# Transformer layer with memory-augmented attention on one core: the layernorm of the next tile issued a chunk ahead, the gates with the constants, the second-layer weight loads later

## The chip, the cores and the metric

The kernel runs on one core of a Trainium2 chip. The metric is the device time of one execution in microseconds (us). TensorE (PE in the profile, PEld for its weight loads) does the matmuls, ScalarE (ACT) exponentials, gelu and copies, VectorE (DVE) and GpSimd (POOL) the elementwise work, and SyncE (SP) issues nearly all transfers.

## The reference

The input is x with 2048 tokens of 576 values, in bfloat16. Both blocks are pre-normalised and added to their input:

```
h  = x + A(layernorm(x))          # attention with a memory, 32 heads of 18
h2 = h + B(layernorm(h))          # gelu(y @ w1 + b1) @ w2 + b2, 4608 wide
# A: q,k,v = y@wq, y@wk, y@wv; four segments of 512 tokens, in order
logits = q k^T * 18**-0.5 + causal mask          # within the segment
a_dot  = softmax(logits) v
a_mem  = (phi(q) M) / (phi(q) z + 1e-6)          # phi(t) = t+1 if t>0 else exp(t)
o      = g * a_mem + (1-g) * a_dot               # g = sigmoid(beta), one a head
M, z   = M + phi(k)^T v, z + sum(phi(k))         # after each segment
A      = concat(o) @ wo
```

## The kernel before

The tokens are cut into 8 chunks of 256, each of two tiles of 128. Streams written as Python generators describe the work. `stream_P` (one for each tile position `tl`) loads a tile of x, normalises it (`layernorm`: L307 statistics, L311 and L312 on VectorE, the power L317 on GpSimd, L320 on VectorE), transposes it into `xT` and makes q, k and v from it (L300 and L301 with `wqkv`; evictions L383, L386, L388, L391). For the first two chunks the transposes are matmuls (L327, L408) with a copy behind them (L365, L411); later they are DMA transposes (L132). `stream_M` sums phi(k) with v into the memory. `stream_A` does the attention of a chunk in 80 visits: 16 score matmuls (L489), one exp over four banks (L495), the causal mask on GpSimd (L499), 16 small matmuls with v (L518), then the division (L554 to L563) and, from chunk 2 on, the memory part (L528 to L548). `stream_B` transposes the attention output `o_nat` into `xT`, multiplies by `wo` (L635), adds x (L637), and normalises again. `stream_F1` is the first layer (L731, eviction L733, gelu L741) and loads `w1` anew for each chunk in nine groups of 512 columns, into two buffers and, early on, into the unused `hT` buffer; `stream_F2` is the second layer (L767) with `w2` held in `w_sb`.

A planner inside the kernel runs these streams while the program is built. Each operation has an engine, an assumed duration, the operations that it depends on and a due time (the planner's clock plus a value of `SLACK`). An engine that is free takes, of its operations that are ready, the one with the earliest due time; TensorE's operations come from the streams in a fixed priority, with L790 to L795 choosing between the attention streams and the two layers. Where nothing is ready and the first layer has not begun, a filler matmul is issued that nothing reads (L805). The order found in this way is what each engine then executes, strictly in order; the assumed durations have no part in the execution. Transfers use eight semaphores in turn, so SP can issue a transfer only when the eighth before it has landed. Transfers on SP also stand in the planned order.

The buffers that matter here: `x_p[tl]` and `xn1[tl]` (the loaded tile and its normalised form) are single for each tile position; there are three `xT` buffers, and three PSUM banks with `ox` as a fourth where attention doesn't hold it. In `stream_P` before, chunk c is loaded and normalised when its turn has come:

```
yield need(lambda: c < 3 or c - 2 - (c + 1) % 2 in done_A, idle=False)
...
if c > 1:
    load_x(t, xt, xk, SLACK["xp"])
if c > 0:
    layernorm(who, xt[:], xk, xn1[tl], xnk, False, SLACK["lnp"])
```

The gates (L278 to L290: an exp on ScalarE, then seven VectorE operations that make g, 1-g and the masked g) are issued when both tiles of chunk 0 have their q, k and v. `beta` is loaded by a DMA that GpSimd issues (L258). The loads of `w2` and of three groups of `w1` stand in a list `later`, from which `stream_A` takes one at each visit (L593).

Of the kernel before, what the change touches and what calls it, by code (L numbers as in the profile page):

```python
# [8 lines left out]
ACT = mybir.ActivationFunctionType  # L9
# [7 lines left out]
def kernel(  # L17
# [40 lines left out]
    def sbuf(name, shape, dt=BF16):  # L58
# [7 lines left out]
    TP, TB = 2, 1  # L66
    NEVER = 1e9
    TABLE_LOAD = 1.283
    SLACK = dict(head=0, lnp=5.5, lnb=9.5, pow=-8.5, apply=8, ek_k=23, relu_k=40, min_k=5, add_k=9, mz=5, exp=13.5,
                 ek=7.5, relu=7.5, min=9.5, add=-6.5, hb=11.5, gelu=3.5, finish=0.5, mem=-20.5, sum=-7, out=22,  # L70
                 hd=9.5, xp=-15.5, xb=2, t_x=9.5, t_q=74.5, t_k=25.5, t_o=4, t_h=30.5, w1=3, w2=30, hc=21, evict=0,
                 qk=-13, ot=-13, mask=10.5, lead=1.25, balance=21)
    ops = []
    now, dma_free, table = 0.0, 0.0, "exp"
    free_at = {"PE": 0.0, "SP": 0.0, "ACT": 0.0, "DVE": 0.0, "POOL": 0.0}
    port_until = {"DVE": 0.0, "POOL": 0.0}
    queue = {e: [] for e in free_at}
    writer, readers = {}, {}

    class Op:  # L80
        start, end = None, NEVER

        def __init__(self, eng, dur, issue, preds, due, table=None, after=None):
            self.eng, self.dur, self.issue, self.preds, self.due, self.table = eng, dur, issue, preds, due, table
            self.made = len(ops)
            self.after = after

        def seen(self, eng):
            return self.end if self.eng == eng else self.end + LAT[self.eng]

        def ready(self):
            return max((o.seen(self.eng) for o in self.preds), default=0.0)

    def preds_of(rd, wr):
        out = [writer[k] for k in rd if k in writer]
# [4 lines left out]
        return out  # L100

    def ready(eng, rd=(), wr=()):
        return max((o.seen(eng) for o in preds_of(rd, wr)), default=0.0)

    def note(o, rd, wr):
        for k in wr:
            writer[k] = o
            readers[k] = []
        for k in rd:
            readers.setdefault(k, []).append(o)  # L110
# [43 lines left out]
    class Slots:  # L154


        def __init__(self, name, n):
            self.free = [(name, i) for i in range(n)]

        def when(self):  # L160
            return min((ready("PE", (), [k]) for k in self.free), default=NEVER)

        def take(self):
            k = min(self.free, key=lambda k: ready("PE", (), [k]))
            self.free.remove(k)
            return k

# [48 lines left out]
    banks["ox"] = ox  # L216
    bank_slots = Slots("bank", 3)
    bank_slots.free.append("ox")
    LATER, AHEAD = 0, 5
    f_slots = bank_slots  # L220
    xT_slots = Slots("xT", 3)

# [14 lines left out]
    def memset(eng, dur, ap, value, key, slack=0.0):  # L237
        e = nc.vector if eng == "DVE" else nc.gpsimd
        op(eng, dur, lambda: e.memset(ap, value), (), [key], slack)
# [6 lines left out]
        load_x(2 + tl, x_b[tl], ("x_b", tl))  # L246
    weights(wo_t, slice(0, D), A_wo, "wo")

    def constants():
        op("POOL", 0.75, lambda: make_identity(nc, ident[:]), (), ["ident"])  # L250
        op("DVE", 0.27, lambda: nc.vector.memset(pq[:], 0.0), (), ["pq"])
        memset("DVE", 0.06, mhalf[:], -0.5, "mhalf")
        for tl in range(2):
            memset("DVE", 0.09, xn1[tl][:, D:XW], 0.0, ("xn1", tl, "pad"))
        for tl in range(2):
            memset("DVE", 0.46, qk_pads[tl][:, :, Dh:32], 0.0, ("qk", tl, "pad"))
        memset("POOL", 1.53, wqkv[64:KTAIL, 4, :], 0.0, "wqkv_pad")
        op("POOL", 0.75, lambda: nc.gpsimd.dma_start(out=beta_bc[:], in_=A_beta.partition_broadcast(P)), (), ["beta"])  # L258
        for j in range(2):
            memset("DVE", 0.09, v_augs[j][:, :, Dh:E], 1.0, ("v1", j))  # L260
        for tl in range(2):
            layernorm(f"p{tl}", x_p[tl][:], ("x_p", tl), xn1[tl], ("xn1", tl), False, -5)
        for j in range(2, 6):
            memset("DVE", 0.14, v_augs[j][:, :, Dh:E], 1.0, ("v1", j), slack=4)
        memset("DVE", 0.09, maskcol[:], 0.0, "maskcol", slack=5)
        for i in range(4):
            memset("DVE", 0.09, maskcol[32 * i:32 * i + Dh, :], 1.0, "maskcol", slack=5)
        for j in range(2):
            memset("POOL", 0.45, phik_pads[j][:, :, Dh:32], 0.0, ("phik", j, "pad"), slack=5)
        for j in range(2):  # L270
# [7 lines left out]
    def gates():  # L278
        op("ACT", 0.25, lambda: nc.scalar.activation(out=g_bc[:], in_=beta_bc[:], func=ACT.Exp, scale=-1.0), ["beta"], ["g"],
           slack=2, table="exp")  # L280
        op("DVE", 0.18, lambda: nc.vector.tensor_scalar(out=g_bc[:], in0=g_bc[:], scalar1=1.0, scalar2=None, op0=ALU.add), (), ["g"],
           slack=3)
        op("DVE", 0.36, lambda: nc.vector.reciprocal(out=g_bc[:], in_=g_bc[:]), (), ["g"], slack=3)
        op("DVE", 0.19, lambda: nc.vector.tensor_scalar(out=omg_bc[:], in0=g_bc[:], scalar1=-1.0, scalar2=1.0, op0=ALU.mult, op1=ALU.add),
           ["g"], ["omg"], slack=3)
        for i in range(4):
            src = g_bc[32 * i:32 * i + 32, :].rearrange("p (g i) -> p g i", i=4)[:, :, i:i + 1]
            op("DVE", 0.4, lambda i=i, src=src: nc.vector.tensor_scalar(
                out=gmzm[32 * i:32 * i + 32, :, :], in0=src.to_broadcast([32, G, Dh]), scalar1=maskcol[32 * i:32 * i + 32, :],
                scalar2=None, op0=ALU.mult), ["g", "maskcol"], ["gmzm"], slack=20)  # L290


    MM = 1 / 2400.0

# [51 lines left out]

    def stream_P(tl):
        who = f"p{tl}"
        for c in range(NCH):
            t = 2 * c + tl  # L350
            yield need(lambda: c < 3 or c - 2 - (c + 1) % 2 in done_A, idle=False)
            xt, xk, xnk = (x_b[tl], ("x_b", tl), ("xn1", tl)) if c == 1 else (x_p[tl], ("x_p", tl), ("xn1", tl))
            if c > 1:
                load_x(t, xt, xk, SLACK["xp"])
            if c > 0:
                layernorm(who, xt[:], xk, xn1[tl], xnk, False, SLACK["lnp"])
            yield need(None, xT_slots, idle=False)
            kx = xT_slots.take()
            xTt = xT[kx[1]]
            if c < TP:  # L360
                yield need(None, bank_slots, [xnk, "ident"], [])
                b = bank_slots.take()
                bank = banks[b]
                op("PE", 0.28, lambda bank=bank: transposes5(xn1[tl], bank), [xnk, (*xnk, "pad"), "ident"], [b])
                op("ACT", 0.69, lambda bank=bank, xTt=xTt: nc.scalar.copy(out=xTt[:], in_=tview(bank)), [b], [kx])  # L365
                bank_slots.give(b)
            else:
                dma_t(KT, xTt[:], xn1[tl][:], [xnk, (*xnk, "pad")], [kx], SLACK["t_x"])
            qk = qk_pads[tl]
            va = v_augs[t % 6]  # L370
            qkk, vk = ("qk", tl), ("v", t % 6)
# [41 lines left out]
            half_P.add((c, tl))  # L413
            if (c, 1 - tl) in half_P:
                done_P.add(c)
                if c == 0:
                    gates()
            if c >= NCH - 2:
                continue
            if c > 0:  # L420
# [144 lines left out]
    def stream_A():  # L565
# [9 lines left out]
        for v in range(len(visits) + 1):  # L575
# [10 lines left out]
            if v >= 1:  # L586
                slot, (c, qt, gh, first, last, units) = back.pop(0)
                own = 2 * (c % 2) + qt
                parts = [(0, 1), (2, 3)] if sum(kt == own for _, kt in units) > 2 else [(0, 1, 2, 3)]
                for part in parts:  # L590
                    yield need(None, None, [("pt", slot, n) for n in part] + value_keys(c, units), ["ox"])
                    weighted(c, units, part, slot, first and part[0] == 0)
                if later and c >= LATER:  # L593
                    later.pop(0)()
                if c > 1 and first:
                    yield need(None, bank_slots, ["pq"])
                    b = bank_slots.take()
# [183 lines left out]
    def step():  # L781

        for e in ("SP", "ACT", "DVE", "POOL"):
            if free_at[e] <= now:
                can = [o for o in queue[e] if o.ready() <= now]
                if can:
                    begin(min(can, key=lambda o: (o.due, o.made)))
# [67 lines left out]
```

## Time and profile before

| what | value |
|---|---|
| median of 3 runs | 482.85 us (481.77 to 485.1) |
| span of the profiled execution | 481.9 us |
| mean granted TensorE clock | 0.996 |
| busy PE, PEld | 471.6 and 369.1 us |
| busy DVE, ACT, POOL | 283.4, 290.0 and 206.8 us |
| moved by DMA | 80.97 MB, mean 168 GB/s |

The profile is of one execution; its span goes from the first to the last instruction, and the time of that execution is not shown apart from it. Busy times are shares of that span. A matmul's record lasts longer than the distance to the next one, since matmuls are pipelined, so the distance from start to start is what a group of matmuls costs.

### The profile page before, as it was taken

To read this page: it belongs to the slowest core of one execution; us is meant where nothing else is said; L and a number is where in the kernel's file an instruction comes from. 1 tells how busy PE (TensorE), PEld (TensorE's weight loads), DVE (VectorE), ACT (ScalarE), POOL (GpSimd) and SP (SyncE) were. 2 spreads that over 40 slices of the span, in tenths; PEclk is the share of its full clock that TensorE was granted. 3 is DMA by queue.
4 is the path that set the end of the run, shared out by engine and by line. 5 is a ranking of instruction groups with operands and counts; after the bars stand their busy time and mean duration, and the time that the engine had idled before them with its cause. 6 is when DMAs were issued, how large, how long until landed. Compare 5 with 4: busy or idle time off the path is not lost.

```text
span 481.9 us, 14443 instructions
## 1 busy us (share of the span) xinstructions
PE 471.6 (98%) x6098; PEld 369.1 (77%) x6098; DVE 283.4 (59%) x688; ACT 290.0 (60%) x205; POOL 206.8 (43%) x291
## 2 busy tenths in 40 slices
PE   8999999799999999999999999999999999999997
PEld 5668778467788878676887878768888778888885
DVE  5798776757776647676546654857534643534311
ACT  2678889763786969468237968658546867122210
POOL 6567552666755246776204353677304251100000
PEclk9999999899999999999999999999999999999999
DMA  8993759576894657499854655787854655755411
GB/s 237 291 337 113 172 147 252 112 139 163 164 215 147 167 160 197 107 197 232 191 174 125 168 152 153 160 145 172 221 171 130 149 151 155 194 173 161 135 38 50
DMA packets 117345, 80.97 MB, mean 168 GB/s; under 512 B 56392, under 2 KB 115232, under 8 KB 117280
## 3 DMA queue, kind: packets, MB, share of 16 engines
q1 hardware_dynamic: 117248, 80.04, 65.9%
q8 instruction: 48, 0.79, 0.7%
q14 instruction: 17, 0.14, 0.1%
q0 software_dynamic: 32, 0.01, 0.1%
HBM read 60.10 MB, written 7.08 MB: 139 GB/s over the span
## 4 chain that ended last, share of the span: by engine, by line
PE 88%; DMA 7%; DVE 2%; SPq 1%; ACT 1%; POOL 0%; issue 0%; ACTq 0%; DVEq 0%; POOLq 0%
PE bank L300 36%; PE bank L767 26%; PE bank L301 9%; PE ox L518 6%; PE st L489 5%; DMA xT<-xn 2%; DMA x_p<-in_A_x_dram 2%; PE ox L767 2%; DMA wqkv<-in_A_wv_dram 2%; PE ox L300 1%; DMA w1g<-in_B_b_dram 1%; ACT pt L495 1%; PE bank L447 1%; PE bank L541 1%; PE bank L805 1%; DMA xT<-o_nat 1%
## 5 line engine op out<-in xcount | busy, mean ns | idle before, releaser
L495 ACT ACTIVATE pt<-st 128x2048 bf16<-128x2048 f32 x80 | 150.2, 1878 | 61.9 <-PE st L489 61.6
L767 PE MATMUL bank<-w_sb,hT 128*128 128x288 bf16 x1080 | 155.7, 286 | 0.0
L300 PE MATMUL bank<-xn2T,w1g 128*128 128x256 bf16 (+1 forms) x1040 | 146.3, 269 | 0.0
L733 DVE CAST hT<-bank 128x512 bf16<-128x512 f32 x126 | 86.7, 690 | 86.9 <-PE bank L301 85.8
L767 PEld LDWEIGHTS <-hT 128*128 128x128 bf16 x1152 | 109.6, 98 | 27.9 <-issue 0.8
L499 POOL TENSOR_SCALAR_AFFINE_SELECT pt<-pt 128x512 bf16<-128x512 bf16 x128 | 81.0, 646 | 82.5 <-ACT pt L495 81.9
L300 PEld LDWEIGHTS <-w1g 128*128 128x128 bf16 x1104 | 101.4, 97 | 17.0
L741 ACT ACTIVATE hT<-hT 128x4608 bf16<-128x4608 bf16 (+3 forms) x22 | 65.9, 2996 | 67.1 <-DVE hT L733 67.0
L301 PE MATMUL bank<-xn2T,w1g 65*128 65x256 bf16 (+1 forms) x260 | 70.4, 271 | 0.1
L300 PE MATMUL bank<-wqkv,xT 128*128 128x432 bf16 x252 | 57.2, 349 | 2.6 <-DMA xT<-xn 2.1
L300 PEld LDWEIGHTS <-xT 128*128 128x128 bf16 x384 | 34.8, 98 | 27.1 <-DMA xT<-xn 2.4
L518 PEld LDWEIGHTS <-pt 128*128 128x128 bf16 x1280 | 43.6, 96 | 5.8 <-POOL pt L499 0.2
L518 PE MATMUL ox<-v_aug,pt 128*128 128x19 bf16 x1280 | 45.8, 172 | 0.1
L563 POOL TENSOR_TENSOR o_nat<-t,t 128x288 bf16<-128x288 f32 x24 | 19.6, 815 | 32.4 <-DVE t L562 32.2
L489 PE MATMUL st<-QT,KT 32*128 32x128 bf16 x1280 | 32.2, 217 | 0.7 <-ACT pt L495 0.7
L533 POOL TENSOR_TENSOR pq<-ek,pq 128x512 bf16<-128x512 bf16 x24 | 28.1, 1170 | 10.2 <-DVE ek L531 8.3
L771 DVE TENSOR_TENSOR ot<-bank,hc 128x288 bf16<-128x288 f32 x30 | 13.7, 457 | 30.0 <-PE bank L767 29.2
L489 PEld LDWEIGHTS <-KT 32*128 32x128 bf16 x1280 | 18.6, 92 | 14.7 <-issue 12.9
L301 PEld LDWEIGHTS <-w1g 65*128 65x128 bf16 x276 | 26.9, 97 | 3.5 <-DMA w1g<-in_B_b_dram 0.4
L317 POOL TENSOR_TENSOR rstd_b<-rstd_b,mhalf 128x1 f32<-128x1 f32 x16 | 8.8, 552 | 44.6 <-DVE rstd_b L312 44.6
L383 ACT CAST qk_pad<-bank 128x432 bf16<-128x432 f32 x31 | 15.9, 522 | 16.9 <-PE bank L301 12.6
L637 DVE TENSOR_TENSOR h_t<-bank,x_b 128x288 f32<-128x288 f32 x32 | 14.6, 457 | 13.5 <-PE bank L301 13.1
(99 smaller groups left out, 499.8 us busy)
## 6 DMA issues: line engine op xcount, KB each, us to landing
w1g<-in_B_w_dram SPq DMA_DIRECT2D x67, 512.0 KB
w_sb<-in_B_w_dram SPq DMA_DIRECT2D x6, 864.0 KB
hd<-h_t SPq DMA_DIRECT2D x16, 288.0 KB
hc<-hd SPq DMA_DIRECT2D x32, 144.0 KB
w1g<-in_B_w_dram SPq DMA_DIRECT2D x67, 64.0 KB
x_b<-in_A_x_dram SPq DMA_DIRECT2D x18, 144.0 KB
hT<-in_B_w_dram SPq DMA_DIRECT2D x5, 512.0 KB
out_dram<-ot SPq DMA_DIRECT2D x16, 144.0 KB
```

What stands on the lines that cost most here:

```text
L300: nc.tensor.matmul(out=out_ap, lhsT=lhsT_of(slice(0, P), k), rhs=rhs_of(slice(0, P), k), start=(k == 0), stop=False)
L301: nc.tensor.matmul(out=out_ap, lhsT=lhsT_of(slice(0, KTAIL), 4), rhs=rhs_of(slice(0, KTAIL), 4), start=False, stop=True)
L383: op("ACT", 0.52, lambda ch=ch, uh=uh, qk=qk: nc.scalar.copy(out=qk[:, 24 * ch:24 * ch + 24, 0:Dh], in_=uh), [b], [(*qkk, ch)])
L489: nc.tensor.matmul(out=st4[:, i, n * P:(n + 1) * P], lhsT=KTs[(c - c % 2 + kt // 2) % 3][rows, g, (kt % 2) * P:(kt % 2 + 1) * P], rhs=QTs[ ...
L495: op("ACT", 1.88, lambda: nc.scalar.activation(out=pt[:], in_=st4[:], func=ACT.Exp, scale=scale), sk, [("pt", slot, n) for n in range(4)], ...
L499: op("POOL", 0.65, lambda n=n: nc.gpsimd.affine_select(out=pt[:, :, n * P:(n + 1) * P], in_=pt[:, :, n * P:(n + 1) * P], pattern=[[0, 4], ...
L518: nc.tensor.matmul(out=oxv[:, 4 * (g % 4) + i, :], lhsT=pts[slot][:, i, n * P:(n + 1) * P], rhs=v_augs[(2 * s0 + kt) % 6][:, 4 * g + i, :] ...
L533: op("POOL", 1.16, lambda: nc.gpsimd.tensor_tensor(out=pq[:], in0=e_g, in1=pq[:], op=ALU.add), ["ek"], ["pq"], slack=SLACK["add"])
L563: op("POOL", 0.8, lambda: nc.gpsimd.tensor_tensor(out=o_dst, in0=t1[:], in1=t2[:], op=ALU.add), ["t1", "t2"], ok, slack=SLACK["sum"])
L733: op("DVE", 0.684, lambda hT=hT, jp=jp, acc=acc: nc.vector.tensor_copy(out=hT[:, 2 * jp:2 * jp + 2, :], in_=acc), [b], [("hT", c % 2, jp)] ...
L741: op("ACT", (f1 - f0) * Q * 0.00083 + 0.18, lambda hT=hT, f0=f0, f1=f1: nc.scalar.activation(out=hT[:, f0:f1, :], in_=hT[:, f0:f1, :], fun ...
L767: nc.tensor.matmul(out=acc, lhsT=hT[:, q, tl * P:(tl + 1) * P], rhs=w2_sb[:, q, hs], start=(q == 0), stop=(q == NF - 1))
```

## The change

The layernorm of chunk c+1 is issued right behind the transposes of chunk c, by a new function `normalise`. Two of its due times get values of their own (`ln1` for chunk 1, `ln2` for chunk 2). `gates` is called within `constants`, between the memsets, with due times from `SLACK["g"]`. The list `later` is drained only while it has more than six entries, or from visit `SLACK["v2"]` = 7 on, which moves the loads of `w2`. Nearly all values of `SLACK` are others. The remaining edits keep results of the planner's own look-ups (`known`, `at`, `latest`) and choose the next operation in a loop, with the same outcome for the same numbers.

```diff
-    SLACK = dict(head=0, lnp=5.5, lnb=9.5, pow=-8.5, apply=8, ek_k=23, relu_k=40, min_k=5, add_k=9, mz=5, exp=13.5,
-                 ek=7.5, relu=7.5, min=9.5, add=-6.5, hb=11.5, gelu=3.5, finish=0.5, mem=-20.5, sum=-7, out=22,
-                 hd=9.5, xp=-15.5, xb=2, t_x=9.5, t_q=74.5, t_k=25.5, t_o=4, t_h=30.5, w1=3, w2=30, hc=21, evict=0,
-                 qk=-13, ot=-13, mask=10.5, lead=1.25, balance=21)
+    SLACK = dict(head=0, lnp=36, lnb=27, pow=-57.5, apply=-0.5, ek_k=14.5, relu_k=13, min_k=31, add_k=-62.5, mz=-16, exp=51,
+                 ek=54.5, relu=-20, min=1.5, add=5.5, hb=-1, gelu=45.5, finish=0.5, mem=-84, sum=36, out=18.5, hd=-58.5,
+                 xp=-104.5, xb=-27, t_x=17.5, t_q=64.5, t_k=-27.5, t_o=-43, t_h=79, w1=56.5, w2=34.5, hc=28.5, evict=0,
+                 qk=-95, ot=-68, mask=-70, lead=9.75, balance=35, g=105, ln1=14, ln2=56.5, v2=7)
...
+        xnk = ("xn1", tl)
+
+        def normalise(c):
+            xt, xk = (x_b[tl], ("x_b", tl)) if c == 1 else (x_p[tl], ("x_p", tl))
+            if c > 1:
+                load_x(2 * c + tl, xt, xk, SLACK["xp"])
+            layernorm(who, xt[:], xk, xn1[tl], xnk, False, SLACK["lnp"] + (SLACK["ln1"] if c == 1 else SLACK["ln2"] if c == 2 else 0))
+
         for c in range(NCH):
             t = 2 * c + tl
             yield need(lambda: c < 3 or c - 2 - (c + 1) % 2 in done_A, idle=False)
-            xt, xk, xnk = (x_b[tl], ("x_b", tl), ("xn1", tl)) if c == 1 else (x_p[tl], ("x_p", tl), ("xn1", tl))
-            if c > 1:
-                load_x(t, xt, xk, SLACK["xp"])
-            if c > 0:
-                layernorm(who, xt[:], xk, xn1[tl], xnk, False, SLACK["lnp"])
             yield need(None, xT_slots, idle=False)
...
                 dma_t(KT, xTt[:], xn1[tl][:], [xnk, (*xnk, "pad")], [kx], SLACK["t_x"])
+            if c + 1 < NCH:
+                normalise(c + 1)
...
             memset("DVE", 0.09, maskcol[32 * i:32 * i + Dh, :], 1.0, "maskcol", slack=5)
+        gates()
         for j in range(2):
...
                 done_P.add(c)
-                if c == 0:
-                    gates()
...
-                if later and c >= LATER:
+                if later and (len(later) > 6 or v >= SLACK["v2"]):
                     later.pop(0)()
```

More of the change, by code (lines that the diff above doesn't have):

```diff
@@ L77 @@
     queue = {e: [] for e in free_at}
-    writer, readers = {}, {}
+    writer, readers, known = {}, {}, {}
     class Op:
-        start, end = None, NEVER
+        start, end, at = None, NEVER, None
         def __init__(self, eng, dur, issue, preds, due, table=None, after=None):
@@ L86, in __init__, with latest @@
             self.after = after
-        def seen(self, eng):
-            return self.end if self.eng == eng else self.end + LAT[self.eng]
         def ready(self):
-            return max((o.seen(self.eng) for o in self.preds), default=0.0)
+            if self.at is None:
+                t = latest(self.preds, self.eng)
+                if t >= NEVER:
+                    return NEVER
+                self.at = t
+            return self.at
+    def latest(preds, eng):
+        t = 0.0
+        for o in preds:
+            s = o.end if o.eng == eng else o.end + LAT[o.eng]
+            if s > t:
+                t = s
+        return t
     def preds_of(rd, wr):
@@ L102, in ready @@
     def ready(eng, rd=(), wr=()):
-        return max((o.seen(eng) for o in preds_of(rd, wr)), default=0.0)
+        return latest(preds_of(rd, wr), eng)
     def note(o, rd, wr):
+        for k in (*rd, *wr):
+            known.pop(k, None)
         for k in wr:
@@ L158, in __init__, with at @@
             self.free = [(name, i) for i in range(n)]
+        def at(self, k):
+            if k not in known:
+                t = ready("PE", (), [k])
+                if t >= NEVER:
+                    return t
+                known[k] = t
+            return known[k]
         def when(self):
-            return min((ready("PE", (), [k]) for k in self.free), default=NEVER)
+            return min((self.at(k) for k in self.free), default=NEVER)
         def take(self):
-            k = min(self.free, key=lambda k: ready("PE", (), [k]))
+            k = min(self.free, key=self.at)
             self.free.remove(k)
@@ L218 @@
     bank_slots.free.append("ox")
-    LATER, AHEAD = 0, 5
+    AHEAD = 5
     f_slots = bank_slots
@@ L247, with gates @@
     weights(wo_t, slice(0, D), A_wo, "wo")
+    def gates():
+        op("ACT", 0.25, lambda: nc.scalar.activation(out=g_bc[:], in_=beta_bc[:], func=ACT.Exp, scale=-1.0), ["beta"], ["g"],
+           slack=SLACK["g"], table="exp")
+        op("DVE", 0.18, lambda: nc.vector.tensor_scalar(out=g_bc[:], in0=g_bc[:], scalar1=1.0, scalar2=None, op0=ALU.add), (), ["g"],
+           slack=SLACK["g"])
+        op("DVE", 0.36, lambda: nc.vector.reciprocal(out=g_bc[:], in_=g_bc[:]), (), ["g"], slack=SLACK["g"])
+        op("DVE", 0.19, lambda: nc.vector.tensor_scalar(out=omg_bc[:], in0=g_bc[:], scalar1=-1.0, scalar2=1.0, op0=ALU.mult, op1=ALU.add),
+           ["g"], ["omg"], slack=SLACK["g"])
+        for i in range(4):
+            src = g_bc[32 * i:32 * i + 32, :].rearrange("p (g i) -> p g i", i=4)[:, :, i:i + 1]
+            op("DVE", 0.4, lambda i=i, src=src: nc.vector.tensor_scalar(
+                out=gmzm[32 * i:32 * i + 32, :, :], in0=src.to_broadcast([32, G, Dh]), scalar1=maskcol[32 * i:32 * i + 32, :],
+                scalar2=None, op0=ALU.mult), ["g", "maskcol"], ["gmzm"], slack=20)
     def constants():
@@ L276, in constants @@
             memset("POOL", 0.55, MZ_blk[j][:], 0.0, ("MZb", j), slack=7)
[L278 to L290, printed above, removed]
     MM = 1 / 2400.0
@@ L784, in step @@
             if free_at[e] <= now:
-                can = [o for o in queue[e] if o.ready() <= now]
-                if can:
-                    begin(min(can, key=lambda o: (o.due, o.made)))
+                best = None
+                for o in queue[e]:
+                    if o.ready() <= now and (best is None or (o.due, o.made) < (best.due, best.made)):
+                        best = o
+                if best:
+                    begin(best)
                     return True
```

## The prediction

> **What bounds the kernel now.** I read the shares of the page first, then the windows of TensorE, its waits, and the timelines around the places that these name. The page:
>
> ```profile
> PE 471.6 (98%) x6098; PEld 369.1 (77%) x6098; DVE 283.4 (59%) x688; ACT 290.0 (60%) x205; POOL 206.8 (43%) x291
> PEclk9999999899999999999999999999999999999999
> ```
>
> TensorE is busy for 98%, no other engine for more than 60%, and its clock is full but for one slice. So the time is a fixed amount of matmul work plus whatever TensorE does besides it. From start to start the groups of matmuls take 0.92 us (five of 432 columns, 12.10 to 13.01 in the timeline), 0.55 us (five of 256 columns, F1), 0.49 us (four of 288, F2), 0.34 us (16 scores) and 0.41 us (16 of L518); times their counts, with the smaller groups, this is 453 us. The span has 481.9, so 29 us are something else: the first matmul starts at 1.3 us, the last one starts 3.5 us before the end, fillers of L805 take 11 us (70 of them), and about 13 us are holes and slow matmuls. Where these lie, first by windows (us, PE busy, PEld, PEclk, DMA share, GB/s for the matmuls of L805; then the whole, with DVE, ACT and POOL in between):
>
> ```profile
> 0.00:20.00 20.00, 7.20 (x47) 5.24 (x47) 1.00 0.92 260
> 20.00:80.00 60.00, 3.67 (x23) 2.04 (x23) 1.00 0.76 206
> ...
> 86.60:93.27 6.67, 3.68 (x56) 2.51 (x55) 6.34 (x17) 5.76 (x4) 4.23 (x8) 1.00 0.55 89
> 93.27:96.68 3.41, 3.41 (x13) 1.65 (x11) 0.89 (x2) 0.52 (x1) 3.13 (x3) 0.50 0.25 48
> 96.68:320.00 223.32, 223.24 (x2924) 172.30 (x2923) 141.68 (x356) 149.01 (x106) 116.36 (x157) 1.00 0.71 166
> ```
>
> After 96.68 us nothing is to be had: TensorE is idle 0.08 us in 223. The fillers and the stretch 86.6 to 96.7 are what a new order can win. The waits of TensorE and the timeline name that stretch:
>
> ```profile
> PE bank L300 <- DMA xT<-xn: 2.1, 1, 2.1
> PE bank L300 <- DMA xT<-o_nat: 1.3, 2, 0.9
> ...
> 88.33 2.54 SPq L132 DMA_TRANSPOSE xT<-xn  x2
> ...
> 90.22 0.30 PE L541 MATMUL bank<-MZ_blk,pq 128*128 128x76 bf16 x4
> 92.61 1.02 PE L300 MATMUL bank<-wqkv,xT 128*128 128x432 bf16 x4 [2.09 <-DMA xT<-xn]
> ...
> 94.74 1.65 PE L300 MATMUL bank<-wqkv,xT 128*128 128x432 bf16 x4
> ```
>
> The reader sees the q/k/v matmuls of chunk 3 stand for a transposed tile, and the same four matmuls then take 1.65 instead of 0.89 us, because the clock is 0.50 from 93.27 to 96.68. The chain of waits says why the tile is late: x_p is asked for at 78.22, the statistics start at 83.32, L320 ends at 88.30, the transpose lands 4.2 us later.
>
> ```profile
> 78.22 5.07 DMA x_p<-in_A_x_dram
> ...
> 88.33 4.24 DMA xT<-xn
> ```
>
> **The change, part by part.** The measure is the lead: the matmul work that stands, in the order that each program issues, between the matmul that last held a transfer back (by its data or by what is ahead of it on SP) and the matmul that uses it, priced by the start-to-start times above.
>
> *Layernorm a chunk ahead.* The same 14 normalisations of x_p and 2 of x_b are issued, with the same loads; only the transpose is left between the release of chunk 3 and its matmuls. For the first tile of chunk 3 the lead was 5 F2 groups, 2 of L635 (0.62), one of scores, 2 half groups of L518 (0.21) and one of L541 (0.23): 4.7 us, and the hole made it 7. Now 11 F1 groups, an F1, scores, a group of L518 and an F2 stand there: 7.8 us. In front of it on SP now stand two pieces of w1 and three x loads (0.4 to 0.5 us each by their rows, 2.3 together), then the transpose with 4.2 us to its landing: 6.5 us, so it is there in time. Of all 26 transposes into xT 16 had a lead under 6.4 us (together 10.8 us short of it), and they cost, from start to start beyond the usual, 1.1 + 2.2 at 86 to 92 us, 0.2 at 221, 0.5 at 323.5: 4.0 us. In the new order 7 are under 6.4, together 3.5 us short. At the same rate (4.0 for 10.8) they cost 1.3. The slow clock cost 0.2 + 0.5 + 0.9 = 1.6 us over the groups from 92.6 to 96.5, and goes with the hole. Sum: -4.0 - 1.6 + 1.3 = -4.3. Bounds: -5.6 if none is late, and at the other end the second rival.
>
> *Fillers.* A filler stands where the order has nothing else. 47 of them are ahead of the first scores in both programs; behind these there were 23 and are 11. 12 times 0.108 us, start to start at full clock: -1.3. Bounds 0 (the place becomes a wait) and -1.3.
>
> *Gates with the constants.* ScalarE's exp of beta (0.23 us, ran at 19.04) becomes its first operation (behind the table load that stands first in both), ahead of the copy of the first transposed tile; one DVE add, reciprocal, product and three more with omg (0.66 + 0.35 + 0.61 + four of 0.4, 3.2 us) go ahead of the first eviction. The exp waits for beta, which GpSimd asks for at 2.92:
>
> ```profile
> 2.92 0.74 POOL L258 DMA_DIRECT2D beta_bc<-in_A_beta_dram  x1
> beta_bc<-in_A_beta_dram POOLq DMA_DIRECT2D x1, 8.0 KB, 5.8
> 7.25 0.69 ACT L365 COPY xT<-bank 128x640 bf16<-128x640 bf16 x1 [5.16 <-PE bank L327]
> 8.00 0.90 PE L300 MATMUL bank<-wqkv,xT 128*128 128x432 bf16 x4
> ...
> 12.10 0.89 PE L300 MATMUL bank<-wqkv,xT 128*128 128x432 bf16 x4 [0.39 <-DMA wqkv<-in_A_wv_dram]
> ```
>
> It lands 5.8 us later, at 8.7. ScalarE then ends the exp at 9.0 and the copy at 9.7; behind it wait the evictions L383 and the other copy. The first q/k/v group starts at 9.7 instead of 8.0, the second at 10.6, the other tile's transposes and five fillers run to 12.4, and the third group starts there instead of at 12.10, where it waited for wv: 1.4 of the 1.7 us vanish behind that load. VectorE does its added work until about 13.5, where the eviction L386 stood at 13.29: +0.3. Bounds 0 and, without the cover of wv, +1.7. The same 3.2 us leave VectorE at 21 to 34 us, where no matmul waited for them; I take nothing.
>
> *Later w2 loads.* The six are issued from the 36th place on SP instead of the 31st; their shortest lead falls from 50 to 42 us, far above the 8.07 us that wv took under a full DMA share. Nothing, both ends.
>
> *Other due times.* The w1 loads have their shortest leads: 5.06 once and 5.15 fourteen times before, and one hole of 0.25 us (346.7). Now four have 4.9 and thirteen 5.15. Between nothing and 4 x 0.25 plus the old one; I take +0.3. The holes of the first 80 us outside the fillers (about 2.4 us, scores and L518 behind exp and mask) may go either way by 1.5; I take 0, since the exp is 1.88 us for 80 operations as before. The planner's caches issue nothing.
>
> Sum: -4.3 - 1.3 + 0.3 + 0.3 = -5.0 us. The profiled execution has a span of 481.9, and the lowest run shown is 481.8, so little lies around it; the median is 0.9 above. 482.85 - 5.0 = 477.85.
>
> [...]
>
> **Rivals.** (1) The gap at 8.0 to 9.7 us halves the clock, as 2.1 us did at 92. 3.4 us at 0.50 are 1.7 us lost in work that the wv load no longer covers: 477.85 + 1.7 = 479.6. For it: nearer to 2.1 than to the 0.9 that did nothing at 87. Against: the cover of 12.10, and TensorE did fillers up to the gap.
>
> (2) The slower side: x loads and stores now pass the transposes on SP, and each transpose needs 7.0 us or more from its release, as the one issued at 83.18 did (lead 6.35, 1.1 late: 7.4). Then 11 leads are short, together 8.7 us: 482.85 - 5.6 - 1.3 + 0.6 + 8.7 = 485.3, and 490.6 at 7.4 (14.0 us). It decides against the change from a need of about 6.8 us (6.7 short). Against: under that rule the old order would have lost 21 us, and lost 4.
>
> (3) The tile was late for another reason than the layernorm, and the hole stays: 482.85 - 1.3 + 0.6 = 482.1. Against: L320 ends at 88.30 and the transpose starts at 88.33.
>
> (4) More is won: no transpose late (-1.3 more) and the early holes fall by 1.5: 475.0.
>
> **How the numbers follow.** Forecast 0.55 (its own range 476 to 480), rival 1 0.14, rival 2 0.12, rival 3 0.05, rival 4 0.14. A change of 1% is 4.8 us, about what a measurement of this kernel tells from none; the bound is 478.0. Below it lie rival 4 and somewhat more than half of the forecast, 0.48 with a little of rival 1; slower than 487.7 is the upper part of rival 2 and what I don't see, 0.08; the rest 0.44. The range runs from 474 (rival 4 and a us) to 483.5 (rival 3, the lower edge of rival 2).
>
> **What would show it.** The clock row at 9 throughout; no wait of TensorE for xT over 0.5 us at chunk 3; 58 matmuls of the filler line; ScalarE's first copy of xT near 9.0, the third q/k/v group near 12.4. The forecast is wrong if waits for xT sum to over 3 us, or if TensorE waits for exp in the first 80 us more than before.

## The result, and the profile after

| what | before | after |
|---|---|---|
| median | 484.42 us (22 executions beside the changed kernel's) | 486.20 us (483.38 to 490.03, 22 executions) |
| ratio | 1 | 1.0048, 95% interval 1.0026 to 1.0069 |
| profiled execution | span 481.9 us, clock 0.996 | span 488.3 us, time 490.03 us, clock 0.993 |

The change makes the kernel slightly slower, 2.3 us by the ratio (1.3 to 3.3 by its interval), where 5.0 us of gain were forecast. The profiled execution is the slowest of the 22, so part of what it shows is its own; a second trace was taken for that reason (below). First the page of the changed kernel, the lines that answer to those of before:

```profile
span 488.3 us, 14408 instructions
...
PE 473.2 (97%) x6086; PEld 369.0 (76%) x6086; DVE 278.9 (57%) x688; ACT 289.7 (59%) x206; POOL 207.0 (42%) x291
...
PEclk9899999999989999999999999999999999999999
```

TensorE has 12 matmuls less (the fillers, 58 instead of 70, as forecast). The slice at half clock (a granted clock of 0.50) near 90 us is gone, and two others are there. The windows of the whole (us, PE busy, PEld, DVE, ACT, POOL, PEclk, DMA share, GB/s) say where time is idle now:

```profile
0.00:20.00 20.00, 16.39 (x120) 10.86 (x121) 11.81 (x47) 5.45 (x10) 8.88 (x23) 0.91 0.90 260
...
80.00:137.00 57.00, 56.73 (x669) 42.59 (x666) 42.94 (x111) 40.05 (x32) 34.32 (x47) 1.00 0.76 159
137.00:145.00 8.00, 5.48 (x61) 3.60 (x58) 2.43 (x7) 5.36 (x4) 0.23 (x1) 0.79 1.33 223
...
250.00:310.00 60.00, 56.95 (x829) 44.72 (x828) 31.44 (x70) 43.94 (x27) 24.97 (x34) 1.00 0.73 177
```

Before, TensorE was idle 0.08 us between 96.7 and 320; now it loses 2.5 us in eight at 137 and 3.1 between 250 and 310, and 80 to 137, where the hole of the fourth chunk (chunk 3 in the prediction) was, is nearly full. TensorE's waits name the new causes:

```profile
PE bank L320 <- DMA w1g<-in_B_w_dram: 3.7, 3, 2.5
PE bank L320 <- ACT xT L388: 2.7, 2, 2.3
...
PE bank L321 <- DMA w1g<-in_B_w_dram: 1.2, 1, 1.2
PE bank L320 <- DMA xT<-o_nat: 0.6, 1, 0.6
...
PE bank L320 <- DMA xT<-xn: 0.3, 1, 0.3
```

The waits for `xT` from a DMA transpose, 3.4 us before, are 0.9. In their place stand 4.9 us of waits for loads of `w1` (at 138, 256, 260 and 303 us) and 2.3 us at the head. The longest, in TensorE's timeline:

```profile
137.83 0.65 PE L790 MATMUL bank<-w_sb,hT 128*128 128x288 bf16 x4
141.00 0.61 PE L320 MATMUL bank<-xn2T,w1g 128*128 128x256 bf16 x4 [2.52 <-DMA w1g<-in_B_w_dram]
141.44 0.28 PE L321 MATMUL bank<-xn2T,w1g 65*128 65x256 bf16 x1
141.61 1.14 PE L320 MATMUL bank<-wo_t,xT 128*128 128x288 bf16 x4
```

After the wait of 2.52 us the clock is 0.50 from 141.60 to 145.02, and the group of `wo` takes 1.14 instead of 0.65 us. SP's own timeline tells what it did before that load:

```profile
127.26 0.38 SPq L704 DMA_DIRECT2D w1g<-in_B_w_dram  x1
...
128.74 2.91 SPq L144 DMA_TRANSPOSE KT<-qk_pad  x2
131.70 1.04 SPq L251 DMA_DIRECT2D x_b<-in_A_x_dram  x1
132.84 0.37 SPq L797 DMA_DIRECT2D out_dram<-ot  x1
133.25 0.44 SPq L779 DMA_DIRECT2D hc<-hd  x1
133.78 0.41 SPq L704 DMA_DIRECT2D w1g<-in_B_w_dram  x1
...
136.60 1.85 SPq L144 DMA_TRANSPOSE QT<-qk_pad  x1
138.54 1.95 SPq L704 DMA_DIRECT2D w1g<-in_B_w_dram  x1
```

The buffer's last reader ended at 131.9. SP came to the load at 133.78, because two transposes of keys, 2.91 us of its time, and three small transfers stood ahead of it. The load then needed 7.2 us until its matmuls ran, with two more transposes right behind it on the queue; in the old order, by the prediction's leads, 5.1 us from release to use had been enough but for one wait of 0.25 us. The tiles that these transposes make are first read at 198 and 212 us.

The old order has the same two key transposes near this place, and no hole:

```profile
124.30 3.05 SPq L132 DMA_TRANSPOSE KT<-qk_pad  x2
128.89 0.39 SPq L681 DMA_DIRECT2D w1g<-in_B_w_dram  x1
```

There SP was done with them at 127.4, the buffer came free at 128.9, the load went out at once and its matmuls ran at 136.52 without a wait. So two transposes in a row are not the trouble by themselves; it is that a buffer comes free while they, and what they pushed back, still hold the queue.

### The profile page after: what moved, and what is told of

Same layout as the page of the kernel before. It is cut to its first block, busy times and chain, and to the rows that moved or that the text cites. A ratio compares the mean times of both kernels' runs of the same rounds, so it can differ in the third digit from the quotient of the medians.

```text
span 488.3 us, 14408 instructions
## 1 busy us (share of the span) xinstructions
PE 473.2 (97%) x6086; PEld 369.0 (76%) x6086; DVE 278.9 (57%) x688; ACT 289.7 (59%) x206; POOL 207.0 (42%) x291
## 4 chain that ended last, share of the span: by engine, by line
PE 83%; DMA 8%; ACT 3%; DVE 2%; POOL 1%; issue 1%; SPq 0%; ACTq 0%; POOLq 0%; DVEq 0%
PE bank L320 34%; PE bank L790 24%; PE bank L321 8%; PE ox L541 6%; PE st L512 5%; DMA w1g<-in_B_w_dram 4%; ACT pt L518 2%; PE ox L790 2%; PE ox L320 2%; DMA xT<-o_nat 1%; DMA beta_bc<-in_A_beta_dram 1%; DMA x_p<-in_A_x_dram 1%; PE bank L564 1%; DMA xT<-xn 1%; PE ox L321 0%
## 5 line engine op out<-in xcount | busy, mean ns | idle before, releaser
L790 PE MATMUL bank<-w_sb,hT 128*128 128x288 bf16 x1080 | 149.9, 286 | 0.0
L320 PE MATMUL bank<-xn2T,w1g 128*128 128x256 bf16 (+1 forms) x1040 | 144.7, 269 | 3.9 <-DMA w1g<-in_B_w_dram 3.7
L320 PEld LDWEIGHTS <-w1g 128*128 128x128 bf16 x1104 | 101.4, 97 | 20.4 <-DMA w1g<-in_B_w_dram 4.6
L764 ACT ACTIVATE hT<-hT 128x4608 bf16<-128x4608 bf16 (+4 forms) x23 | 66.1, 2875 | 52.8 <-DVE hT L756 52.6
L320 PE MATMUL bank<-wqkv,xT 128*128 128x432 bf16 x252 | 56.9, 348 | 3.4 <-ACT xT L388 2.7
L320 PEld LDWEIGHTS <-xT 128*128 128x128 bf16 x384 | 34.9, 98 | 26.6 <-ACT xT L388 3.2
L541 PEld LDWEIGHTS <-pt 128*128 128x128 bf16 x1280 | 42.5, 96 | 6.7 <-issue 0.5
L551 ACT ACTIVATE ek<-QT 128x512 bf16<-128x512 bf16 x24 | 15.1, 628 | 16.1 <-POOL pq L556 10.5
```

The lines of the kernel that those rows point to most:

```text
L320: nc.tensor.matmul(out=out_ap, lhsT=lhsT_of(slice(0, P), k), rhs=rhs_of(slice(0, P), k), start=(k == 0), stop=False)
L541: nc.tensor.matmul(out=oxv[:, 4 * (g % 4) + i, :], lhsT=pts[slot][:, i, n * P:(n + 1) * P], rhs=v_augs[(2 * s0 + kt) % 6][:, 4 * g + i, :] ...
L764: op("ACT", (f1 - f0) * Q * 0.00083 + 0.18, lambda hT=hT, f0=f0, f1=f1: nc.scalar.activation(out=hT[:, f0:f1, :], in_=hT[:, f0:f1, :], fun ...
L790: nc.tensor.matmul(out=acc, lhsT=hT[:, q, tl * P:(tl + 1) * P], rhs=w2_sb[:, q, hs], start=(q == 0), stop=(q == NF - 1))
```

## The theories

Theory A: the head. ScalarE's first instruction waits for beta (until 9.62 us) and holds back the copy of the first transposed tile. Theory B: the weights. Transposes of q and k on SP's queue, placed anew by the changed due times, make the loads of `w1` beside them late. A third question came with the first results: how much the fourth chunk's hole, the forecast's largest term, is worth in an ordinary execution.

In all experiments but the two repeats and the replanned one, the planner runs as it is, and the place of a few chosen operations in the finished order is then changed; all others keep theirs. These kernels have one more line above the functions, so L320 and its like are one higher there. The helper:

```diff
+    def picked(eng, *wr):
+        return sorted((o for o in ops if o.eng == eng and o.wr == wr), key=lambda o: (o.start, o.made))
+    def move(group, t):
+        for i, o in enumerate(group):
+            o.start = t + 1e-4 * (i + 1)
     ...
         for o in sorted(ops, key=lambda o: (o.start, o.made)):
             o.issue()
```

| kernel | median us | ratio to before | 95% interval |
|---|---|---|---|
| changed, gates late | 487.02 | 1.0073 | 1.0047 to 1.0099 |
| changed, beta first | 485.32 | 1.0044 | 1.0015 to 1.0073 |
| changed, transposes late in blocks | 490.64 | 1.0153 | 1.0112 to 1.0194 |
| changed, transposes spread | 481.57 | 0.9962 | 0.9941 to 0.9983 |
| changed, spread and beta first | 481.18 | 0.9955 | 0.9940 to 0.9970 |
| changed, spread and gates late | 481.38 | 0.9980 | 0.9953 to 1.0007 |
| before, fourth layernorm early | 483.33 | 0.9991 | 0.9962 to 1.0019 |
| before, gates early | 484.85 | 1.0043 | 1.0023 to 1.0064 |
| before, both of these | 482.58 | 1.0014 | 0.9983 to 1.0046 |
| before, layernorm ahead, replanned | 495.29 | 1.0263 | 1.0206 to 1.0320 |

The kernel before ran beside each group, with medians of 484.4, 483.4, 482.2 and 482.6 us, so the ratios are what is compared.

## The gates: undone, and beta's load first

```diff
+    move(picked("ACT", "g"), picked("ACT", *[("pt", 0, n) for n in range(4)])[0].start)
+    move(picked("DVE", "g") + picked("DVE", "omg"), picked("DVE", ("KT", 0, 1))[0].start)
+    move(picked("DVE", "gmzm"), picked("DVE", ("KT", 1, 0))[0].start)
```

> The changed kernel (486.2 us) with one thing undone: the eight gate instructions go back to the places they have in the kernel before. ScalarE's exp of beta comes after the first exp of scores, VectorE's add, reciprocal and 1-g after the copy of the second half of the keys, the four masked gates a step later. All else keeps its order. Theory A (head): ScalarE's first instruction waits 7.5 us for beta to land at 9.6, and holds back the copy of the first transposed tile, which makes a gap of 2.3 us ahead of the second query/key/value group and, in part of the executions, a stretch at half clock. Then the gap goes, the first scores start near 17.0 instead of 19.5, and the time is 482.5 to 484.0. Theory B (weights): the loss sits in late loads of the first-layer weights at 138, 256 and 260 us. Then the time stays within 0.7 of 486.2.

Measured: 1.0073, no gain, and 11 of the 12 executions have a stretch at half clock (a mean clock of 0.992 to 0.997, the twelfth 0.999). And with beta's load as GpSimd's first work, `move(picked("POOL", "beta"), -1.0)`:

> The changed kernel with beta's load as the first thing that GpSimd does, ahead of the identity matrix and the pad; the gates stay where the change put them. Theory A says that the landing of beta costs the time and not the gate instructions themselves (0.23 us on ScalarE, about 2 us on VectorE, all at the head): with beta there about 2 us earlier, near 7.5, the gap ahead of the second query/key/value group shrinks from 2.3 us to under 1, and the time is 483 to 484.5. If the instructions themselves are the cost, the gap stays near 2 us and the time within 0.7 of 486.2. Theory B: 486.2 as well.

Measured: 1.0044, 0.2 us from the changed kernel by the ratio, far inside the interval. Beta lands 5.0 us after it is asked for (6.7 in the changed kernel), TensorE's waits for the copies fall from 2.7 to 0.3 us, and the time does not follow. Theory A falls in its strong form. Why, a pair of heads shows best, both without the holes further on: the spread kernel (below) with the gates early and with the gates late. TensorE's timeline with the gates early:

```profile
8.71 0.27 PE L832 MATMUL bank<-pq 128*128 128x256 bf16 x1
10.07 0.90 PE L321 MATMUL bank<-wqkv,xT 128*128 128x432 bf16 x4 [1.08 <-ACT xT L389]
...
10.99 0.89 PE L321 MATMUL ox<-wqkv,xT 128*128 128x432 bf16 x4
...
12.74 0.89 PE L321 MATMUL bank<-wqkv,xT 128*128 128x432 bf16 x4
```

And with the gates late:

```profile
8.88 0.90 PE L321 MATMUL bank<-wqkv,xT 128*128 128x432 bf16 x4
...
10.38 0.89 PE L321 MATMUL ox<-wqkv,xT 128*128 128x432 bf16 x4 [0.41 <-DMA wqkv<-in_A_wk_dram]
...
12.51 0.89 PE L321 MATMUL bank<-wqkv,xT 128*128 128x432 bf16 x4 [0.22 <-DMA wqkv<-in_A_wv_dram]
```

With the gates late the first group starts 1.2 us earlier, and the second and third then wait for the key and value weights. The third group, 12.51 against 12.74, gives 0.2 us. That is the cover which the forecast named. In the trace of the changed kernel with late gates the wait for the key weights was 1.9 us, a stretch at half clock followed it too (the clock row has 8 tenths in the slice from 12.2 to 24.4 us), and the third group stood at 13.62, against 14.33 with early gates and a stretch.

## The transposes of q and k

The eight are the key and query transposes of chunks 4 and 6, counted from 0 (the first chunks of the third and fourth segment; the expectations call them the third and fourth chunk). First they were moved away in two blocks, four behind the loads at 150 us and four at 265:

```diff
+    turns = [o for o in ops if o.eng == "SP" and o.wr[:1] and o.wr[0][0] in ("QT", "KT")]
+    move([o for o in turns if 124 < o.start < 135], 151.0)
+    move([o for o in turns if 233 < o.start < 241], 256.0)
```

> The changed kernel with one thing moved: eight transposes of queries and keys on the DMA queue of SyncE (four in the third chunk, four in the fourth, whose tiles TensorE first reads 50 to 80 us later) go behind the loads of first-layer weights that they stand ahead of now. Theory B (weights): the load whose buffer came free at 131.9 was issued at 133.8, behind two of these transposes, landed 7.2 us later beside two more, and TensorE stood 2.7 us for it at 138, then ran a stretch at half clock (1.6 us); 0.7 and 0.8 us went the same way at 256 and 260. Then these holes close and the time is 482 to 484. Theory A (head only): within 0.7 of 486.2. If the loads are late for another reason (their own 4.9 us from issue to landing), the holes stay.

Measured: 1.0153, slower still, and the trace says why. The holes at 138, 256 and 260 are gone; TensorE has new ones right behind each block. SP's timeline at the first block:

```profile
153.54 1.24 SPq L145 DMA_TRANSPOSE QT<-qk_pad  x1
154.83 2.58 SPq L145 DMA_TRANSPOSE KT<-qk_pad  x1
157.50 1.26 SPq L145 DMA_TRANSPOSE QT<-qk_pad  x1
158.81 1.33 SPq L145 DMA_TRANSPOSE KT<-qk_pad  x1
...
161.34 0.39 SPq L705 DMA_DIRECT2D w1g<-in_B_w_dram  x1
```

TensorE's two longest waits in the same kernel (us in all, times, longest):

```profile
PE bank L321 <- DMA xT<-o_nat: 4.2, 2, 3.8
PE bank L321 <- DMA w1g<-in_B_w_dram: 3.1, 1, 3.1
```

The hole went along with the transposes: the load of `w1` that was next on the queue went out at 161.34, and TensorE stood for it from 162.4 to 165.5. Behind the second block it stood 3.8 us, from 275.0 to 278.8, for a transpose of `o_nat`. The time missed the expectation by more than 6 us, but what made it slower is the mechanism of theory B at two other places. So the same eight were put singly, each behind another load of `w1`:

```diff
+    third = [o for o in turns if 124 < o.start < 135]
+    fourth = [o for o in turns if 233 < o.start < 241]
+    for group, times in ((third, {("QT", 0, 0): 168.25, ("KT", 1, 0): 172.5, ("QT", 0, 1): 180.7, ("KT", 1, 1): 184.85}),
+                         (fourth, {("KT", 0, 0): 252.75, ("QT", 0, 0): 267.15, ("KT", 0, 1): 274.95, ("QT", 0, 1): 279.25})):
+        for o in group:
+            o.start = times[o.wr[0]]
```

> The changed kernel (486.2 us) with the same eight transposes of queries and keys moved later on SyncE's queue, but one at a time, each behind another load of first-layer weights, and none in a block of four. In the run where they were moved as two blocks, the holes at 138, 256 and 260 us were gone and new ones of 3.2 and 4.0 us stood right behind the blocks. Theory B (these transposes, several together, make the loads next to them late): neither the old holes nor the new ones, 482.5 to 484.5. Theory B' (one such transpose ahead of a weight load is enough): four to eight holes of 0.5 to 1 us, 486 or more. Theory A (head only): 486.2 within 0.7.

Measured: 481.57 us, 0.9962, below the expected range. Against 1.0048 of the changed kernel eight transposes are worth 0.86%, 4.2 us (with the two intervals taken together, 2.7 to 5.6). The waits for `w1` fall from 4.9 to 0.3 us:

```profile
PE bank L321 <- DMA w1g<-in_B_w_dram: 0.3, 1, 0.3
```

And the windows that were idle are nearly full:

```profile
137.00:145.00 8.00, 8.00 (x109) 6.39 (x107) 6.13 (x16) 6.07 (x6) 5.40 (x7) 1.00 0.75 180
...
250.00:310.00 60.00, 59.33 (x850) 45.93 (x849) 32.61 (x79) 43.69 (x29) 30.51 (x43) 1.00 0.79 184
```

One transpose between two loads costs little: of the waits for `w1` the one of 0.3 us, at 174.3, is all that is left. SP in this kernel:

```profile
172.77 0.39 SPq L705 DMA_DIRECT2D w1g<-in_B_w_dram  x1
...
174.75 1.25 SPq L145 DMA_TRANSPOSE KT<-qk_pad  x1
...
176.92 0.37 SPq L705 DMA_DIRECT2D w1g<-in_B_w_dram  x1
```

Two more on this base, the first with `move(picked("POOL", "beta"), -1.0)`, the second with the gates' moves of above:

> The one before with beta's load as GpSimd's first work as well. Theory B with a small share for the head (beta first gave 0.9 us by the medians): 481.5 to 484, 0.3 to 1.2 below the one before. If the head's gap is set by the weights' landing alone: no difference to the one before within 0.7.

Measured: 0.9955, which is not told from 0.9962, but the best of all: faster than the kernel before by 2.2 us (1.4 to 2.9) and than the changed kernel by 4.5.

> The changed kernel with the eight query and key transposes spread out (481.6 us) and the gates back where the kernel before has them, so that the head is judged without the holes at 138 and 256 us. Theory A (the wait for beta costs 2 us at the head): 479.3 to 480.3. Theory A' (the key weights land at 9.8 to 11.0 and cover it): within 0.7 of 481.6, with the gap now ahead of the second query/key/value group instead of the first.

Measured: 481.38 us, 0.9980. Theory A', that the landing of the key weights covers the wait for beta, holds against the 2 us of theory A: late gates are 0.9 us slower than early ones in this order by the ratios (0.8 us faster to 2.5 slower), so no difference can be told.

## A second trace of both kernels

> The changed kernel once more for a second trace: the first one is of an execution of 490.0 us, with two stretches at half clock, 3.8 above the median of 486.2. Expected are the same holes in the first-layer loads at 138, 256, 260 and 303 us, and at the head a gap ahead of the first query/key/value group of 2.0 to 2.6 us. Theory B: the hole at 138 is there whatever the clock does.

Measured: 486.26 us, and the holes are there, smaller: waits of 0.7 and 1.3 us at 136 to 139 with a half clock behind them (mean clocks of 0.70 from 138.5 to 142 us and 0.83 from 142 to 146), 0.5 at 254, 0.6 at 274. At the head TensorE waits 1.4 us for the copy, below the expected 2.0 to 2.6, the first scores start at 17.75 instead of 19.47, and there is no half clock before 130. Near 303 there is no wait for `w1`, so the one of 1.2 us was the first execution's own.

> The kernel before once more for a second trace. The first has the fourth chunk's hole at 86 to 96 us at 3.2 us of waits and 1.6 us of half clock; the trace of the kernel before with early gates has there only one wait of 1.6 us. If the hole was particular to that execution, the second trace shows 1.0 to 2.0 us of waits and no half clock between 84 and 97 us, at a time of 481.5 to 484; if it belongs to the kernel, 3 to 5 us again.

Measured: 482.35 us. Here the forecast's first term meets its limit:

```profile
89.00 0.66 PE L300 MATMUL bank<-wo_t,xT 128*128 128x288 bf16 x4 [1.87 <-DMA xT<-o_nat]
...
91.58 0.30 PE L541 MATMUL bank<-MZ_blk,pq 128*128 128x76 bf16 x4
91.72 0.89 PE L300 MATMUL bank<-wqkv,xT 128*128 128x432 bf16 x4
...
93.52 0.89 PE L300 MATMUL bank<-wqkv,xT 128*128 128x432 bf16 x4 [0.24 <-DVE t L548]
```

In the trace that the forecast read, the group of `wo` waited 0.90 us and the q/k/v group 2.09 more, and then 1.6 us went to half clock. Here the first wait is longer, the second is not there, and the clock stays. The same stretch costs 2.1 us of waits instead of 4.6 with its slow clock. And the wait that is left is for the transposed attention output, `o_nat`; for the normalised tile, which the forecast's first term is about, TensorE does not wait here at all.

## Parts of the change in the kernel before

The fourth chunk's layernorm alone, early:

```diff
+    for tl, t in ((0, 66.0), (1, 70.0)):
+        move(picked("SP", ("x_p", tl))[2:3], 60.0 + 0.01 * tl)
+        st = picked("DVE", f"stp{tl}")
+        move(st[9:12], t)
+        move(picked("POOL", f"stp{tl}")[3:4], t + 1.5)
+        move(picked("DVE", ("xn1", tl))[3:4], t + 3.0)
```

> The kernel before (484.4 us) with the change's main idea alone, and for the one chunk where its trace shows a hole: the loads, statistics and normalisation of the fourth chunk's two token tiles run some 20 us earlier on SyncE's queue, VectorE and GpSimd; nothing moves on TensorE or ScalarE, and the gates, weights and all due times stay. The forecast's first term says that the hole at 86 to 96 us (1.1 + 2.2 us of waits and 1.6 us from half clock) closes: 479.5 to 481. If layernorm is not what that hole waits for, or the extra VectorE work ahead of the exp and copies of the chunk before costs as much, it stays at 483.5 to 485.

Measured: 483.33 us, 0.9991: nothing that can be told from no change. The hole does close, the wait for `o_nat` included (why that one goes too, no run separates), and none of the 12 executions has a stretch at half clock (mean clocks of 0.999 and 1.000), where 12 of the 29 of the kernel before beside it have one (0.992 to 0.996). But a smaller hole opens where VectorE now does the statistics first:

```profile
71.94 0.40 PE L490 MATMUL st<-QT,KT 32*128 32x128 bf16 x16
73.36 0.43 PE L448 MATMUL bank<-v_aug,phik_pad 128*128 128x76 bf16 x8 [1.02 <-DVE hT L714]
...
91.57 0.89 PE L301 MATMUL bank<-wqkv,xT 128*128 128x432 bf16 x4
```

The gates alone, early, by the same kind of moves the other way:

> The kernel before (484.4 us) with the eight gate instructions alone moved to where the change has them: ScalarE's exp of beta as its first instruction, VectorE's part between the two normalisations of the first chunk. Theory A: the wait for beta delays the first query/key/value group from 8.0 to 10.4 us, 486.4 to 488.4. Theory A' (the landing of the key weights, which takes until 9.8 to 11.0 in the runs so far, covers most of that wait): 484.4 to 485.6, though the trace shows the wait for beta.

Measured: 484.85 us, 1.0043 beside a kernel before of 483.4 us, that is 2.1 us slower (1.1 to 3.1), the lower edge of theory A's range. Its trace has the wait of 2.4 us for the copy. Whether the head itself or a knock-on at the fourth chunk costs it, this was to tell, with both moves at once:

> The kernel before with two of the parts together: the fourth chunk's layernorm early (0.9991 of the kernel before by itself, and no stretch at half clock in its 12 executions) and the gates early (1.0043 by themselves, 8 of 12 executions with such a stretch). In the changed kernel, early gates cost nothing once the other holes are gone. If the early gates cost at the head itself, this is 1.003 to 1.006 of the kernel before; if they cost only by way of the fourth chunk's hole and its half clock, it is 0.997 to 1.001.

Measured: 482.58 us, 1.0014 (0.9983 to 1.0046). In its trace TensorE waits 2.0 us for the copy, and still the first scores start at 17.54, as they did at 17.58 without the early gates. That speaks for the knock-on, and so does the clock: 8 of 12 executions have a stretch at half clock (mean clocks of 0.995 and 0.996) with the gates early and 3 of 12 (0.996) with the layernorm early as well. Against it, the scores start at 18.19 with the gates alone and at 16.75 and 17.14 in the two traces of the kernel before. The interval reaches into both expectations, so how early gates slow the old order is left open.

Last, the idea without the due times: `normalise` in the kernel before, planned anew with its old `SLACK`.

```diff
                 dma_t(KT, xTt[:], xn1[tl][:], [xnk, (*xnk, "pad")], [kx], SLACK["t_x"])
+            if c + 1 < NCH:
+                normalise(c + 1)
```

> The kernel before (484.4 us) with one part of the change alone: each token tile's loads and layernorm are issued to the planner a chunk ahead, and all due times and the gates stay, so that the planner orders everything anew. Its plan ends 10.6 us later than that of the kernel before, because layernorm with its old due times goes ahead of VectorE's evictions, and 13 more fillers are planned. Theory: the new due times are a needed part of the change, and this is 488 to 496. Rival: issuing ahead is good by itself, and this is 480 to 484.

Measured: 495.29 us, 1.0263. TensorE's waits in it are spread over gelu (`ACT hT`), evictions and transposes:

```profile
PE bank L773 <- ACT hT L747: 3.4, 2, 2.2
PE bank L301 <- DMA xT<-o_nat: 1.5, 2, 0.9
...
PE bank L301 <- DVE v_aug L397: 1.2, 2, 0.8
```

It has 83 fillers instead of 70 and two stretches at half clock (a mean clock of 0.993). Issued ahead with the old due times, the layernorms push other work back; the change needs new due times.

## Why the prediction was wrong

*Layernorm a chunk ahead (-4.3).* The wait that this term was about does go: with the release a chunk earlier, what is left of it at the fourth chunk is 0.6 us or less in every trace of the changed kernel and its variants. The size was off, because it was taken from an execution with more than its share: 4.6 us there, 2.1 in the second trace (all but 0.2 of it for `o_nat`), and 0.4 (a gain of 1.8 to a loss of 0.9) for that part alone. Its 1.6 us of half clock were counted in full (the group of 1.65 us is the q/k/v group behind the one that waited, which took 1.02), but of the 92 executions of the kernel before beside the experiments only 25 have a stretch anywhere. What stays late, 1.3 by the forecast, was about right: 0.4, 0.4 and 0.7 us, from start to start, at 88, 221 and 277.

*Fillers (-1.3).* Right: 58 of them, and 10.5 us from start to start in the spread kernel with late gates against 11.2 and 11.8 in the two traces of before, 0.7 to 1.3 us.

*Gates (+0.3).* In the profiled execution rival 1 came true: beta landed at 9.6, not 8.7, TensorE stood 2.3 us and the clock was halved from 11.90 to 15.31, so the third q/k/v group stood at 14.33, not 12.4. The kernel with the transposes in blocks shows the same (2.3 us, and 8 tenths in the clock row's slice from 12.3 to 24.6 us); the second trace and the spread kernel, with waits of 1.4 and 1.1 us, do not. It is not the rule: the spread kernel has the same head, and 11 of its 12 executions have no stretch at all. Nor does putting the gates back in it gain anything that can be told. So nothing speaks against the +0.3, but it rests on a single number of 5.8 us for beta's landing that did not hold (5.8 to 6.7 us in six traces with the load at that place).

*Later w2 loads (0).* No wait for them in any trace.

*Other due times (+0.3).* This is the step that failed. It priced the loads of `w1` by the matmul work between a buffer's release and its next use, 4.9 us at the least. At 138 us that lead is 6.4 us, more than most, and the load was late by 2.5, because the lead does not count what SP does in between. The step asked where the loads of `w1` were moved and never where the transposes of q and k went. The diff shows it: `t_k` falls from 25.5 to -27.5 and `w1` rises from 3 to 56.5, so of two that are ready, issued to the planner at the same moment, the key transpose now goes ahead of the load, where the load went first before. With the eight transposes spread the term is gone: it measures 4.2 us. How much of this is SP's time and how much is loads that take longer to land (7.2 us for the one issued at 133.8, 5.5 for the one at 256.1), no run separates.

The changed kernel without that term is 1.8 us below before (0.9962), where -4.3 - 1.3 + 0.3 was forecast; with the 4.2 us it is the 2.3 us of loss. So of the 7.3 us between forecast and result 3.9 are the step that failed, and the rest is gain that the other terms promised and did not bring, the first above all. Undoing the layernorm alone in the changed order was not tried. Neither of the two signs that the forecast had named for being wrong appeared: the waits for `xT` from a DMA transpose sum to 0.9 us, and the waits for exp in the first 80 us are 0.4 us after 0.7. Both signs watched the terms that the sum had, and none watched the loads of `w1`.

Rival 2 looked on the right queue but at the wrong passengers: the transposes into `xT` were hardly late; the transposes of q and k made others late. Rivals 3 and 4 did not happen.

## What to carry to other kernels

When due times or priorities change, list for every in-order queue what now stands directly ahead of each transfer that is needed soon, the unhurried ones most of all: a DMA transpose took about 1.25 us of its queue here (medians of 1.21 to 1.38 in the first traces of both kernels), and two of them just ahead of a load with 6.4 us of lead, with more behind it, made it 2.5 us late. Put such work singly between the hurried loads. And price a hole from more than one execution before it becomes the largest term of a sum: one trace had 4.6 us where the next had 2.1.

## What the runs showed of the hardware

Half clock (0.50) comes in stretches of 3.41 us in the first traces of both kernels, from 93.27 us before and from 11.90 and 141.60 after, and once for about 6.9 us in the kernel with the transposes in blocks (mean clocks of 0.99, 0.50 and 0.65 in the three windows of 4 us from 274 us on). It comes in some executions of the same program and not in others. Of the changed kernel's 22 executions 9 have a mean clock of 1.000 (median 484.5 us), 10 one of about 0.996, one such stretch as in the first trace of before (487.0), and 3 one of about 0.993, two stretches as in its own first trace (489.9): 2.5 and 2.9 us more, where 3.41 us at half speed are 1.7 by themselves. With the transposes spread 11 of 12 have none, and with only the early gates in the old order 8 of 12 have one, against 5 of the 29 of the kernel before beside it.

The two stretches of the changed kernel's first trace start 129.7 us apart, which is 38.0 times the 3.41 us of one; what sets the starts, one pair does not show.

No single length of gap decides. Waits of 1.9 us (the changed kernel with late gates, 9 us), 2.1 (before, 92 us), 2.3 (the changed kernel's head) and 2.5 us (138 us) were followed by a stretch; waits of 1.9 (before, second trace, 89 us), 2.0 and 2.4 us (the heads of the two kernels with early gates in the old order) were not. Why one is and another is not, no run here shows.
